# First product of the second network for two of three token blocks in seven half products, with converted weights and some results kept in scratch memory

## The chip, the cores and the metric

The kernel runs on one core of a Trainium2 chip. A core has TensorE (matrix products, results into the 8 banks of PSUM), VectorE, ScalarE and GpSimd (elementwise work), and SP, whose queue issues most transfers between the chip's memory and SBUF. The metric is the device time of one execution: 579.11 us before the change, the median of three (578.52 to 579.46).

## What is computed

Attention over 2 batches, 8 heads and 768 positions; its output is laid out as 1536 tokens by 512. Two networks follow:

```python
x = attention(q, k, v)                # 1536 x 512
h = ((x @ w1) * (x @ w2)) @ w3        # w1, w2: 512 x 1024, w3: 1024 x 1024
x = h @ w_out                         # 1024 x 512, the first network's result
h = x @ w_in                          # 512 x 2048: the first product of the second network
g = h * np.clip(h + 3.0, 0.0, 6.0) / 6.0
y = g @ w_out2                        # 2048 x 512: its second product
```

The results are float32. The weights arrive as 64-bit numbers.

## The kernel before

Tokens go in three blocks (j) of 512. A float32 operand is held as two tiles, a high part (`F32R`) and the remainder, and a product of two operands is three passes of TensorE (high x high, low x high, high x low), so a 128 x 128 by 128 x 512 term is three matmuls (`products`, L299).

Weights are converted on the chip (`convert`, L228): a load into a staging buffer (`raws`, four of them), two instructions on ScalarE (L261, L267), two on VectorE that assemble a float32 in one of four buffers `cs` (L276, L280), then the high part on ScalarE (L284) and the low part on GpSimd (L288), both into a slot of the big tile `arena` or of one of the later tiles.

The first network runs block by block, eight steps each: `ab` (L532) makes two products of 12 matmuls in banks 4 and 5, multiplies them on VectorE and splits the result, and `acc1` (L548) accumulates it through the merged weights into banks 0 to 3. `x2_out` (L553) turns a finished block into the second network's input, four tiles with high and low parts. The attention of later blocks runs between these steps, in banks 6 and 7.

The second network takes 16 column tiles for each block. `hu` (L567) makes one tile of `h`, 4 terms or 12 matmuls in bank 4 or 5; ScalarE adds 3 and cuts at zero (L575), VectorE applies the minimum and multiplies (L579), and `split` (L517) makes the high part on ScalarE (L519) and the low part on VectorE (L524). `acc2` (L586) multiplies the tile of two steps earlier by its output weights, 12 matmuls, three into each of banks 0 to 3, which accumulate over 16 tiles. `y_out` (L591) writes a finished block. All 32 weight tiles of the second network stay in SBUF; the first eight slots of these (`late`) open when the attention's buffers close.

The order of the instructions is written by a planner. Each operation is put down with an engine, an assumed duration, a due time, the keys it reads and writes, and `Graph.schedule` (L100) lays out a list for each engine: what is ready goes, the earliest due first. On the chip each engine works through its list in order and waits where an operand isn't there.

Of the kernel before, what the change touches and what calls it, by code (L numbers as in the profile page):

```python
# [22 lines left out]
F32 = mybir.dt.float32  # L23
# [32 lines left out]
A_LATE = A_W2 + 8  # L56
N_RAW, N_C = 4, 4
# [105 lines left out]
def build(tc, qd, kw, vw, kt, vt, consts, wp_in, w12_in, w2_in, out):  # L163
# [5 lines left out]
    psp = tc.tile_pool(name="ps", bufs=1, space=bass.MemoryType.PSUM)  # L169
    pool = main.__enter__()  # L170
    pp = psp.__enter__()
    ar = pool.tile([P, A_N, 2, TB], F32R, name="arena")
# [27 lines left out]
    def open_tiles(cm, name, side, s0):  # L200
# [19 lines left out]
    def take(name, n):  # L220
        t = turn[name] % n
        turn[name] += 1
        return t
# [4 lines left out]
    def convert(due, src, s, pieces=1, banks=None, lo="pool", n_raw=N_RAW):  # L228

# [12 lines left out]
        if n_conv[0] <= LOD:  # L242
            lo = "dve"
        bk = banks[take("cb", len(banks))] if banks else None
        for i in range(pieces):
# [24 lines left out]
            else:  # L270
# [12 lines left out]
            g.op("act", 180 + 450 * f, due - 2 * us,  # L283
                 lambda cf=cf, e=e: nc.scalar.activation(out=slot(s)[:, 0, e], in_=cf, func=AF.Copy),  # L284
                 [kci] + [kc] * (pieces > 1), [("t", s, 0)])
            eng = nc.gpsimd if lo == "pool" else nc.vector
            g.op(lo, 60 + 1230 * f if lo == "pool" else 150 + 540 * f, due - 1.3 * us,
                 lambda cf=cf, e=e, eng=eng: eng.tensor_tensor(  # L288
                     out=slot(s)[:, 1, e], in0=cf, in1=slot(s)[:, 0, e].bitcast(F32), op=ALU.subtract),
                 [kci, ("t", s, 0)] + [kc] * (pieces > 1), [("t", s, 1)], True)  # L290
# [8 lines left out]
    def products(due, terms, out_ap, b, reads, start=True, stop=True, writes=None):  # L299


        def fn():
            n = 0
            for lhs, rhs in terms:
                for a, c in PASSES:
                    nc.tensor.matmul(  # L306
                        out=out_ap, lhsT=lhs(a), rhs=rhs(c),
                        start=start and n == 0, stop=stop and n == 3 * len(terms) - 1,
                    )
                    n += 1  # L310

        g.op("pe", 684 * len(terms), due, fn, reads, [("bank", b)])
# [254 lines left out]
    def hu(due, j, i, swin):  # L567
# [6 lines left out]
        t, u, gs = ta[n % 2], tg[n % 2], A_G + n % 3  # L574
# [11 lines left out]
    def acc2(due, i, gs, swout, cs_=range(4)):  # L586
        for c in cs_:
            terms = [(wslice(gs, c * P), lambda h: slot(swout)[:, h, :])]
            products(due + c, terms, bank[c], c, both(swout) + both(gs), i == 0, i == NFC2 - 1)

    def y_out(due, j, c, halves=False):  # L591
# [3 lines left out]
        for n, eng in enumerate(("act", "dve") if halves else ("act",)):  # L595
# [3 lines left out]
            def fn(eng=eng, e=e):  # L599
                if eng == "act":  # L600
                    nc.scalar.activation(out=o[:, e], in_=bank[c][:, e], func=AF.Copy, scale=1.0 / 6.0)
                else:
                    nc.vector.tensor_scalar(
                        out=o[:, e], in0=bank[c][:, e], scalar1=1.0 / 6.0, scalar2=None, op0=ALU.mult
                    )
# [4 lines left out]
            g.op(eng, 480 if w == TB else 290, due, fn, [("bank", c)], [("c", c % N_C, n)] + [("c", c % N_C)] * (n == 0))  # L610
# [34 lines left out]
    with tc.manual_schedule():  # L645
# [63 lines left out]
        for i in range(2):  # L709
# [3 lines left out]

        slots = [A_LATE + i for i in range(8)] + [w12(i) for i in range(2 * NFC)] + [A_WP + i for i in range(NFC)]
        g.op("late", 1, 0, lambda: open_tiles(att_cm, "late", "right", A_LATE), (),
             att_keys + [k for i in range(8) for k in both(A_LATE + i)])
        wslots = [(slots[2 * i], slots[2 * i + 1]) for i in range(NFC2)]

        acc1_last = pend
        order = [(j, i) for j in range(NBLK) for i in range(NFC2)]  # L720
        done = []
        first = True
        conv_next = 0

        def conv_to(n):
            nonlocal conv_next
            while conv_next < min(n, NFC2):
                i = conv_next
                dl = d2_of(i)
                convert(dl - 8 * us, w2_in[i], wslots[i][0])  # L730
                convert(dl - 4 * us, w2_in[NFC2 + i], wslots[i][1])
                conv_next += 1

        def d2_of(i):
            return T2 + (2 * i) * GRP


        conv_to((8 + 2 * NFC) // 2)
        for n, (j, i) in enumerate(order):
            gs = hu(due, j, i, wslots[i][0])  # L740
            due += GRP
            done.append((j, i, gs))
            if first:
                acc1(due, acc1_last[1], acc1_last[2])
                x2_out(due, acc1_last[0])
                due += GRP
                first = False
                conv_to(NFC2)
            if n >= 2:
                pj, pi_, pg = done[n - 2]  # L750
                acc2(due, pi_, pg, wslots[pi_][1])
                due += GRP
                if pi_ == NFC2 - 1:
                    for c in range(4):
                        y_out(due, pj, c)
        for c in range(4):
            for pj, pi_, pg in done[-2:]:
                acc2(due, pi_, pg, wslots[pi_][1], [c])
                due += GRP / 4
            y_out(due, NBLK - 1, c, c == 3)  # L760
        for _, i in g.schedule():
            g.ops[i][3]()
        for cm in reversed(pools):
            cm.__exit__(None, None, None)
        psp.__exit__(None, None, None)
# [68 lines left out]
```

## Time and profile before

| | |
|---|---|
| median of three runs | 579.11 us |
| span of the profiled execution | 577.1 us |
| outside the span | 2.0 us (of the median) |
| TensorE busy | 549.4 us, 3080 matmuls recorded |
| VectorE, ScalarE, GpSimd busy | 308.4, 258.7, 161.2 us |
| share of the chain of waits on TensorE | 84% |

The trace is of one execution, whose own time is known by its span alone. Instructions are named by engine, line and tiles (`out<-in`, without buffer numbers). A matmul's busy time overlaps with its neighbours', so the pace of TensorE is read from the starts of successive groups. A VectorE or GpSimd instruction that has begun and waits for its turn at SBUF counts as busy.

### The profile page before, as it was taken

The numbers are of one execution on the slowest core, as the hardware profiler recorded it, in microseconds if no ns is written. First come the engines' busy times: TensorE is split into PE (matmuls) and PEld (weight loads), VectorE is DVE, ScalarE is ACT, GpSimd is POOL, SyncE is SP. The second block draws the span as 40 slices with busy tenths as digits, with TensorE's granted clock in tenths as the row PEclk, the third lists the DMA queues.
The fourth block names the chain that finished last, engine by engine and source line by source line (L and its number), as shares of the span: only waits on it lengthen the run. The fifth ranks groups of instructions, "written<-read, shape, count | busy, mean of one in ns | idle before, by whom it ended". The sixth has DMA issues, their size and how long they took to land.

```text
span 577.1 us, 7851 instructions
## 1 busy us (share of the span) xinstructions
PE 549.4 (95%) x3080; PEld 448.1 (78%) x3080; DVE 308.4 (53%) x416; ACT 258.7 (45%) x435; POOL 161.2 (28%) x130
## 2 busy tenths in 40 slices
PE   0689999999999999999999999999999999999997
PEld 0467778887878887878888888888888888888885
DVE  5899978857793336478976862222222222222221
ACT  2788877446531122386777652223222122322222
POOL 0578656794430022254633440000000000000000
PEclk9989999999999999999999999999999999999999
DMA  8999773655443010025553310000100000100002
GB/s 310 380 359 337 214 272 110 203 183 203 149 133 108 21 50 28 1 76 172 187 181 114 110 36 2 1 1 1 73 0 1 0 1 0 74 0 1 0 1 73
DMA packets 27709, 60.16 MB, mean 104 GB/s; under 512 B 2441, under 2 KB 11913, under 8 KB 27673
## 3 DMA queue, kind: packets, MB, share of 16 engines
q1 hardware_dynamic: 27528, 59.53, 31.6%
q8 instruction: 24, 0.39, 0.3%
q10 hardware_dynamic: 144, 0.13, 0.1%
q14 instruction: 13, 0.10, 0.0%
HBM read 54.90 MB, written 3.15 MB: 101 GB/s over the span
## 4 chain that ended last, share of the span: by engine, by line
PE 84%; DMA 9%; DVE 4%; ACT 1%; SPq 1%; issue 1%; ACTq 0%; DVEq 0%
PE bank L306 81%; DMA raw<-in_wp_dram 7%; PE bank L489 1%; DMA kall<-in_kw_dram 1%; PE bank L474 1%; PE bank L427 1%; DVE c L280 1%; DMA raw<-in_w_dram 1%; SPq L226 1%; DVE sc L438 0%; DVE st L458 0%; DVE bank L276 0%; ACT sc L455 0%; DVE arena L506 0%; DVE st L459 0%
## 5 line engine op out<-in xcount | busy, mean ns | idle before, releaser
L306 PE MATMUL bank<-arena 128*128 128x512 f32 x1344 | 323.1, 395 | 0.9 <-DVE arena L640 0.7
L306 PEld LDWEIGHTS bank<-arena 128*128 128x128 f32 x1344 | 251.6, 189 | 56.3 <-issue 1.4
L579 DVE SCALAR_TENSOR_TENSOR tg<-ta,bank 128x512 f32<-128x512 f32 x48 | 33.1, 689 | 141.8 <-ACT ta L575 141.8
L306 PE MATMUL bank<-arena,w 128*128 128x512 f32 x432 | 103.4, 392 | 0.0
L575 ACT ACTIVATE ta<-bank,three 128x512 f32<-128x512 f32 x48 | 33.0, 688 | 144.7 <-PE bank L306 144.7
L306 PEld LDWEIGHTS bank<-arena,w 128*128 128x128 f32 x432 | 80.5, 188 | 17.1 <-issue 0.3
L288 POOL TENSOR_TENSOR arena<-c,arena 128x512 fp32r<-128x512 f32 (+1 forms) x50 | 65.4, 1321 | 64.6 <-ACT arena L284 64.6
L519 ACT ACTIVATE arena<-tg 128x512 fp32r<-128x512 f32 x72 | 45.5, 632 | 62.0 <-DVE tg L543 31.3
L524 DVE TENSOR_TENSOR arena<-tg,arena 128x512 fp32r<-128x512 f32 x68 | 52.0, 764 | 34.0 <-ACT arena L519 33.9
L276 DVE SCALAR_TENSOR_TENSOR c<-c,raw 128x512 uint32<-128x512 uint32 x48 | 49.4, 1048 | 3.4 <-ACT raw L267 3.3
L280 DVE SCALAR_TENSOR_TENSOR c<-raw,c 128x512 uint32<-128x512 uint32 x48 | 48.3, 1019 | 0.2
L267 ACT ACTIVATE raw<-raw 128x512 uint32<-128x512 uint32 (+1 forms) x72 | 47.2, 660 | 0.0
L261 ACT ACTIVATE c<-raw 128x512 f32<-128x512 f32 x48 | 31.8, 667 | 19.4 <-DMA raw<-in_w_dram 16.7
L543 DVE TENSOR_TENSOR tg<-ta,bank 128x512 f32<-128x512 f32 x24 | 16.5, 686 | 44.9 <-PE bank L306 43.7
L454 POOL TENSOR_TENSOR sc<-sc,st 128x960 f32<-128x960 f32 x12 | 21.9, 1829 | 51.5 <-DVE st L452 51.5
L306 PE MATMUL bank<-late,arena 128*128 128x512 f32 x144 | 34.6, 389 | 0.0
L306 PE MATMUL bank<-w,arena 128*128 128x512 f32 x144 | 34.6, 389 | 0.0
L306 PE MATMUL bank<-arena,late 128*128 128x512 f32 x144 | 34.4, 389 | 0.0
L284 ACT ACTIVATE arena<-c 128x512 fp32r<-128x512 f32 (+1 forms) x50 | 29.8, 605 | 4.8 <-DVE c L280 2.8
L306 PEld LDWEIGHTS bank<-arena,late 128*128 128x128 f32 x144 | 27.0, 188 | 5.6
L306 PEld LDWEIGHTS bank<-late,arena 128*128 128x128 f32 x144 | 27.0, 188 | 5.6
L306 PEld LDWEIGHTS bank<-w,arena 128*128 128x128 f32 x144 | 27.0, 188 | 5.6
(48 smaller groups left out, 369.0 us busy)
## 6 DMA issues: line engine op xcount, KB each, us to landing
raw<-in_w_dram SPq DMA_DIRECT2D x48, 512.0 KB, 3.8
raw<-in_wp_dram SPq DMA_DIRECT2D x22, 512.0 KB, 7.2
vall<-in_vw_dram SPq DMA_DIRECT2D x24, 192.0 KB, 4.0
raw<-in_vt_dram SPq DMA_DIRECT2D x6, 512.0 KB, 4.1
qst<-in_q_dram SPq DMA_DIRECT2D x12, 256.0 KB, 3.6
out_dram<-c SPq DMA_DIRECT2D x11, 256.0 KB, 2.2
kall<-in_kw_dram SPq DMA_DIRECT2D x8, 320.0 KB
raw<-in_kt_dram SPq DMA_DIRECT2D x3, 512.0 KB
```

The source lines that it names most:

```text
L261: lambda uf=uf, wf=wf: nc.scalar.activation(out=uf, in_=wf[:, :, 1], func=AF.Copy, scale=2.0**-112),
L267: lambda lw=lw: nc.scalar.activation(out=lw, in_=lw, func=AF.Copy, scale=2.0**-29 * (1 - eps), bias=7.5 * eps - 0.5),
L276: lambda ui=ui, lw=lw: nc.vector.scalar_tensor_tensor(out=ui, in0=ui, scalar=3, in1=lw, op0=ALU.logical_shift_left, op1=ALU.bitwise_or),
L280: lambda ci=ci, ui=ui, hw=hw: nc.vector.scalar_tensor_tensor(out=ci, in0=hw, scalar=0x80000000, in1=ui, op0=ALU.bitwise_and, op1=ALU.bitwi ...
L284: lambda cf=cf, e=e: nc.scalar.activation(out=slot(s)[:, 0, e], in_=cf, func=AF.Copy),
L288: lambda cf=cf, e=e, eng=eng: eng.tensor_tensor(out=slot(s)[:, 1, e], in0=cf, in1=slot(s)[:, 0, e].bitcast(F32), op=ALU.subtract),
L306: nc.tensor.matmul(out=out_ap, lhsT=lhs(a), rhs=rhs(c), start=start and n == 0, stop=stop and n == 3 * len(terms) - 1,)
L454: lambda: nc.gpsimd.tensor_tensor(out=s8, in0=s8, in1=wide(0), op=ALU.subtract), [("st", i2)], skeys)
L519: g.op("act", 630, due, lambda: nc.scalar.activation(out=slot(s)[:, 0, :], in_=src_ap, func=AF.Copy), [src_key], [("t", s, 0)])
L524: lambda: eng.tensor_tensor(out=slot(s)[:, 1, :], in0=src_ap, in1=slot(s)[:, 0, :].bitcast(F32), op=ALU.subtract), [src_key, ("t", s, 0)], ...
L575: g.op("act", 600, due, lambda: nc.scalar.activation(out=t, in_=bank[b], func=AF.Relu, bias=three), [("bank", b), "three"], [("ta", n % 2)])
L579: lambda: nc.vector.scalar_tensor_tensor(out=u, in0=t, scalar=6.0, in1=bank[b], op0=ALU.min, op1=ALU.mult), [("bank", b), ("ta", n % 2)], ...
```

## The change

Token blocks 0 and 1 and the two halves of the inner dimension (512 = 2 x 256) form a 2 x 2 arrangement with two column tiles of `w_in` (tiles q and q + 8). Where the kernel before made four tiles of `h` from eight half products of 6 matmuls, the changed one makes seven half products of sums and differences of the operands (Strassen's scheme, in the form with fewer sums), for each of the 8 values of q. Block 2 is still computed by `hu`.

- `sums_of_x`: before the loop, GpSimd adds high and low parts of eight tiles of x, VectorE forms eight differences, and they are split again into the slots `A_W1` (of the first network's weights).
- `w_in_group(q)`: two converted tiles of `w_in`; GpSimd forms four half-width sums or differences of them in `tmps` 6 and 7; all four tiles are split into the slots `A_W2`. The plain two are also stored to scratch memory (`wi`).
- The loop: per q the half products 1, 5, 6, 2, 7, 4, 3 go to three of banks 4 to 7. Bank A collects 1, 6, 7 and 4, and ScalarE copies it out after 1, 6 and 7 (`copied`); bank B takes 2, bank C takes 5 and 3. VectorE adds the copies to the banks (`added`) for three of the four results; `gated` applies the activation and the split. Block 0's two results are accumulated in the next q (`acc2`, 24 matmuls); block 1's two are stored to scratch (`gj`).
- The 16 output weight tiles are converted in place in the staging buffers, stored to scratch (`wo`), and fetched into 12 slots as needed.
- After the loop: block 2, whose `w_in` tiles are fetched back from scratch, and last the accumulation of block 1 in banks 4 to 7, whose 16 results are fetched back.

The number of instructions goes from 418 to 466 on VectorE, 438 to 486 on ScalarE and 132 to 180 on GpSimd; SP issues 253 transfers instead of 153.

```diff
-        for i in range(8):
+        for i in range(n):
             tiles[s0 + i] = p2.tile([P, 2, TB], F32R, name=f"{name}{i}")
+        for i in range(n_tmp):
+            tmps[i] = p2.tile([P, TB], F32, name=f"{name}_f{i}")
...
+    def spill(due, key, src_fn, reads):
+        d = spilled[key]
+        g.op("sp", 1300, due, lambda: nc.sync.dma_start(out=d, in_=src_fn()), reads, [key])
+
+    def fetch(due, s, key):
+        d = spilled[key]
+        g.op("sp", 1300, due, lambda: nc.sync.dma_start(out=slot(s).bitcast(F32), in_=d), [key], both(s))
+
+    def convert_out(due, src, key, lo="pool"):
+
+        r, c, parts = to_f32(due, src)
+        e, f, cf, keys = parts[0]
+        w = raws[r].bitcast(F32R).rearrange("p (two n) -> p two n", two=2)
+        kr = [("raw", r)]
+        to_hi_lo(due, 1, lambda: cf, keys, lambda: w[:, 0, :], lambda: w[:, 1, :], kr, kr, lo)
+        spill(due, key, lambda: raws[r].bitcast(F32).rearrange("p (two n) -> p two n", two=2), kr)
...
+        wo_slot = [A_LATE + i for i in range(N_LATE)] + [A_WP + i for i in range(NFC)]
+        n_wo = len(wo_slot)
+        tslot = {n: [A_W1 + 2 * (n - 1) + k for k in range(2)] for n in range(1, 5)}
+        ring = [A_G, A_G + 1, A_G + 2, A_X + NPAIR, A_X + NPAIR + 1]
...
+        def w_in_group(due, q):
+
+            w = [A_W2 + 4 * (q % 2) + i for i in range(4)]
...
+            for out, ko, x, kx, op, y, ky in (
+                ((e, lo), ke, (b, lo), kb, ALU.add, (b, hi), kb),
+                ((e, hi), ke, (e, lo), ke, ALU.subtract, (a, lo), ka),
+                ((f, lo), kf, (a, lo), ka, ALU.subtract, (b, lo), kb),
+                ((f, hi), kf, (a, hi), ka, ALU.subtract, (e, hi), ke),
+            ):
+                tensors(due, *(lambda v=v: v[0]()[:, v[1]] for v in (out, x, y)), op, kx, ky, ko, "pool", 0.5)
+            for i, (x, kx) in enumerate(src):
+                s = w[i]
+                to_hi_lo(due, 1, x, [kx], lambda s=s: slot(s)[:, 0, :], lambda s=s: slot(s)[:, 1, :],
+                         [("t", s, 0)], [("t", s, 1)], "dve" if i == 3 else "pool")
+                if i < 2:
+                    spill(due, ("wi", 2 * q + i), lambda s=s: slot(s).bitcast(F32), both(s))
...
+        PAIRS = {
+            1: (0, 0, [A_X, A_X + 1]), 2: (0, 1, [A_X + 2, A_X + 3]),
+            3: (3, 1, [A_X + NPAIR + 2, A_X + NPAIR + 3]), 4: (1, 1, tslot[4]),
+            5: (2, 0, tslot[1]), 6: (2, 1, tslot[2]), 7: (3, 0, tslot[3]),
+        }
...
+        def copied(due, b, f):
+            g.op("act", 600, due, lambda: nc.scalar.activation(out=tmps[f], in_=bank[b], func=AF.Copy),
+                 [("bank", b)], [("f", f)])
+
+        def added(due, b, f, o):
+            g.op("dve", 690, due,
+                 lambda: nc.vector.tensor_tensor(out=tmps[o], in0=bank[b], in1=tmps[f], op=ALU.add),
+                 [("bank", b), ("f", f)], [("f", o)])
+            return lambda: tmps[o], ("f", o)
...
+        sums_of_x(due)
+        for n in range(NFC2):
+            convert_out(due, w2_in[NFC2 + tile_of(n)], ("wo", n))
+        w_in_group(due, 0)
+        w_in_group(due, 1)
+        prev = []
+        for q in range(NFC):
+            bA, bB, bC = (4 + (3 * q + i) % 4 for i in range(3))
...
+            step(1, bA, True)
+            copied(due, bA, 0)
+            step(5, bC, True)
+            filled()
+            step(6, bA, False)
+            copied(due, bA, 1)
+            filled()
+            step(2, bB, True)
+            h11 = added(due, bB, 0, 3)
+            prev.append((2 * q, gated(due, *h11)))
+            step(7, bA, False)
+            copied(due, bA, 2)
+            h22 = added(due, bC, 2, 4)
+            filled()
+            gated(due, *h22, spilled_as=2 * q + 1)
+            step(4, bA, False)
+            prev.append((2 * q + 1, gated(due, lambda b=bA: bank[b], ("bank", bA))))
+            filled()
+            step(3, bC, False)
+            h12 = added(due, bC, 1, 5)
+            gated(due, *h12, spilled_as=2 * q)
+            if q + 2 < NFC:
+                w_in_group(due, q + 2)
...
+        for m, n in enumerate(order):
+            s = A_W2 + m % 8
+            fetch(due, s, ("wi", n))
+            gs = hu(due, NBLK - 1, s, ring[take("gs", len(ring))])
...
+        for n in range(NFC2):
+            s = A_W1 + n % 8
+            fetch(due, s, ("gj", n))
+            if n < NFC2 - 2:
+                acc2(due, n, s, at[n], b0=4)
```

The names in the pieces of order below: `arena` is the big tile (slots of x, of results and of weights), `bank4` to `bank7` take the first product, `bank0` to `bank3` the second, `w20` to `w27` are the slots `A_W2`, `late_f0` to `late_f7` the buffers `tmps`. A number behind a tile's name with an underscore is only its place in memory.

On TensorE, in the second network of the program before, one group of 12 for `hu` and one for `acc2` alternate:

```order
L306 MATMUL bank4_79<-arena_61 128x512 x12
L306 MATMUL bank0_75<-late5_2059,arena_61 128x512 x3
L306 MATMUL bank1_76<-late5_2059,arena_61 128x512 x3
L306 MATMUL bank2_77<-late5_2059,arena_61 128x512 x3
L306 MATMUL bank3_78<-late5_2059,arena_61 128x512 x3
L306 MATMUL bank5_80<-arena_61 128x512 x12
```

In the changed program, the same engine in the loop at q = 1, from the end of its product 6 (bank A is bank 7):

```order
L338 MATMUL bank7_132<-arena_111,w26_711 128x512 x6
L338 MATMUL bank2_127<-late0_2196,arena_111 128x512 x3
L338 MATMUL bank3_128<-late0_2196,arena_111 128x512 x3
L338 MATMUL bank4_129<-arena_111,w24_709 128x512 x6
L338 MATMUL bank7_132<-arena_111,w27_712 128x512 x6
L338 MATMUL bank0_125<-late1_2197,arena_111 128x512 x3
L338 MATMUL bank1_126<-late1_2197,arena_111 128x512 x3
L338 MATMUL bank7_132<-arena_111,w25_710 128x512 x6
```

Between the first two groups in bank 7 (products 6 and 7) stand 12 matmuls; between the last two (7 and 4) stand six. ScalarE copies the bank in each of these gaps.

On ScalarE, in the program before, near the end of the conversions (second network, block 0):

```order
L575 ACTIVATE ta0_70<-bank4_79,three_74 128x512
L284 ACTIVATE arena_61<-c3_69 128x512
L519 ACTIVATE arena_61<-tg0_72 128x512
L575 ACTIVATE ta1_71<-bank5_80,three_74 128x512
L519 ACTIVATE arena_61<-tg1_73 128x512
```

In the changed program, about a half of q = 1; L823 are the copies out of bank A, L292 the high parts of weights, L838 and L552 the activation and the high part of a result:

```order
L292 ACTIVATE w23_708<-late_f7_2207 128x512
L264 ACTIVATE c1_117<-raw2_114 128x512
L270 ACTIVATE raw1_113<-raw1_113 128x512
L823 ACTIVATE late_f1_2201<-bank7_132 128x512
L552 ACTIVATE arena_111<-tg1_123 128x512
L292 ACTIVATE w26_711<-late_f6_2206 128x512
L270 ACTIVATE raw2_114<-raw2_114 128x512
L292 ACTIVATE w24_709<-c2_118 128x512
L823 ACTIVATE late_f2_2202<-bank7_132 128x512
L838 ACTIVATE ta0_120<-late_f3_2203,three_124 128x512
```

The copies now stand between conversions and high parts of weights, some of which wait for GpSimd (`late_f6`, `late_f7`).

On SP's queue, before the last attention units, in the program before (loads into the staging buffers between the attention's):

```order
L226 DMA raw1_63<-in_w2_dram 128x512
L226 DMA vall2_98<-in_vw_dram 96x512
L226 DMA vall3_99<-in_vw_dram 96x512
L226 DMA raw3_65<-in_w2_dram 128x512
L226 DMA raw2_64<-in_w2_dram 128x512
L226 DMA raw0_62<-in_w2_dram 128x512
L226 DMA kall1_95<-in_kw_dram 128x4x160
```

The same place in the changed program:

```order
L237 DMA vall2_148<-in_vw_dram 96x512
L237 DMA vall3_149<-in_vw_dram 96x512
L309 DMA wo1_64<-raw2_114 128x1024
L237 DMA raw2_114<-in_w2_dram 128x512
L309 DMA wo0_63<-raw1_113 128x1024
L237 DMA raw1_113<-in_w2_dram 128x512
L309 DMA wo3_66<-raw0_112 128x1024
L237 DMA raw0_112<-in_w2_dram 128x512
L309 DMA wo2_65<-raw3_115 128x1024
```

Here each staging buffer is stored (`wo`) before it is loaded again; nine such stores stand ahead of the load of `kall1` that came after three loads before.

## Rows read from the trace of the kernel before

**Rows 1.** The chain of waits in order of time, from 245 us: start us, us, what

```profile
245.41 327.72 PE bank L306 x1443
```

**Rows 2.** The timeline, 350 to 366 us: start us, us, engine, line, operation, tiles, count

```profile
352.63 2.88 PE L306 MATMUL bank<-arena 128*128 128x512 f32 x12
352.89 0.69 ACT L575 ACTIVATE ta<-bank,three 128x512 f32<-128x512 f32 x1 [3.36 <-PE bank L306]
353.62 0.69 DVE L579 SCALAR_TENSOR_TENSOR tg<-ta,bank 128x512 f32<-128x512 f32 x1 [3.36 <-ACT ta L575]
...
355.36 2.88 PE L306 MATMUL bank<-arena,w 128*128 128x512 f32 x12
```

**Rows 3.** The page's head: span; busy us (share of the span) and instructions

```profile
span 577.1 us, 7851 instructions
...
PE 549.4 (95%) x3080; PEld 448.1 (78%) x3080; DVE 308.4 (53%) x416; ACT 258.7 (45%) x435; POOL 161.2 (28%) x130
```

**Rows 4.** Busy time by stretch; columns as in the first line

```profile
core 0: us, PE busy (x) PEld busy (x) DVE busy (x) ACT busy (x) POOL busy (x), PEclk, DMA share, GB/s
0.00:50.00 50.00, 28.71 (x243) 22.32 (x245) 39.39 (x62) 32.64 (x58) 27.56 (x30) 0.97 1.00 350
190.00:220.00 30.00, 30.00 (x221) 24.25 (x221) 11.44 (x18) 5.78 (x9) 4.36 (x3) 1.00 0.11 34
250.00:310.00 60.00, 60.00 (x266) 49.71 (x265) 49.66 (x56) 44.57 (x78) 29.66 (x22) 1.00 0.55 169
```

**Rows 5.** Groups by line and form: busy us, mean ns, idle before

```profile
L519 ACT ACTIVATE arena<-tg 128x512 fp32r<-128x512 f32 x72 | 45.5, 632 | 62.0 <-DVE tg L543 31.3 <-DVE tg L579 30.6
...
L541 ACT ACTIVATE ta<-bank 128x512 f32<-128x512 f32 x24 | 14.3, 594 | 35.4 <-PE bank L306 35.3
...
L288 POOL TENSOR_TENSOR arena<-c,arena 128x256 fp32r<-128x256 f32 x4 | 2.9, 728 | 14.5 <-ACT arena L284 14.5
```

**Rows 6.** The timeline, 297 to 330 us, VectorE and GpSimd

```profile
297.13 2.56 POOL L288 TENSOR_TENSOR w<-c,w 128x512 fp32r<-128x512 f32 x2 [3.13 <-ACT w L284]
...
298.50 0.69 DVE L543 TENSOR_TENSOR tg<-ta,bank 128x512 f32<-128x512 f32 x1 [2.15 <-PE bank L306]
...
301.36 0.68 DVE L280 SCALAR_TENSOR_TENSOR c<-raw,c 128x512 uint32<-128x512 uint32 x1
301.96 1.28 DVE L276 SCALAR_TENSOR_TENSOR c<-c,raw 128x512 uint32<-128x512 uint32 x2
...
323.75 1.60 POOL L288 TENSOR_TENSOR w<-c,w 128x512 fp32r<-128x512 f32 x1 [3.70 <-ACT w L284]
324.13 1.77 DVE L276 SCALAR_TENSOR_TENSOR c<-c,raw 128x512 uint32<-128x512 uint32 x1
...
325.31 1.74 POOL L288 TENSOR_TENSOR arena<-c,arena 128x512 fp32r<-128x512 f32 x1
```

**Rows 7.** Groups by line, 250 to 310 us, VectorE alone

```profile
L280 DVE SCALAR_TENSOR_TENSOR c<-raw,c 128x512 uint32<-128x512 uint32 x20 | 19.8, 1001 | 0.0
L276 DVE SCALAR_TENSOR_TENSOR c<-c,raw 128x512 uint32<-128x512 uint32 x20 | 18.1, 928 | 2.0 <-ACT raw L267 2.0
L524 DVE TENSOR_TENSOR arena<-tg,arena 128x512 fp32r<-128x512 f32 x8 | 9.4, 1171 | 0.5 <-ACT arena L519 0.5
```

**Rows 8.** The timeline of ScalarE, 250 to 310 us

```profile
271.82 0.68 ACT L261 ACTIVATE c<-raw 128x512 f32<-128x512 f32 x1 [1.21 <-DMA raw<-in_w_dram]
272.41 0.58 ACT L541 ACTIVATE ta<-bank 128x512 f32<-128x512 f32 x1
...
279.39 0.60 ACT L541 ACTIVATE ta<-bank 128x512 f32<-128x512 f32 x1 [0.51 <-PE bank L306]
...
295.96 0.57 ACT L541 ACTIVATE ta<-bank 128x512 f32<-128x512 f32 x1
```

**Rows 9.** Transfers by line: KB each, median us from issue to landing

```profile
raw<-in_w_dram SPq DMA_DIRECT2D x48, 512.0 KB, 3.8
...
out_dram<-c SPq DMA_DIRECT2D x11, 256.0 KB, 2.2
```

More of the change, by code (lines that the diff above doesn't have):

```diff
@@ L56 @@
 A_LATE = A_W2 + 8
+N_LATE, N_TMP = 4, 8
 N_RAW, N_C = 4, 4
@@ L282, in convert @@
                  keys + [ku] * bool(banks), [kci] + [kc] * (pieces > 1 and i == 0 and bool(banks)), not banks)
[L283 to L290, printed above, removed]
+            out.append((e, f, cf, [kci] + [kc] * (pieces > 1)))
@@ new lines, in convert @@
+    def convert(due, src, s, pieces=1, banks=None, lo="pool", n_raw=N_RAW):
+        if n_conv[0] < LOD:
+            lo = "dve"
+        r, c, parts = to_f32(due, src, pieces, banks, n_raw)
+        for e, f, cf, keys in parts:
+            to_hi_lo(due, f, lambda cf=cf: cf, keys, lambda e=e: slot(s)[:, 0, e], lambda e=e: slot(s)[:, 1, e],
+                     [("t", s, 0)], [("t", s, 1)], lo)
+    def spill(due, key, src_fn, reads):
+        d = spilled[key]
+        g.op("sp", 1300, due, lambda: nc.sync.dma_start(out=d, in_=src_fn()), reads, [key])
@@ L297, in build, with products @@
     PASSES = ((0, 0), (1, 0), (0, 1))
-    def products(due, terms, out_ap, b, reads, start=True, stop=True, writes=None):
+    def products(due, terms, out_ap, b, reads, start=True, stop=True, skip=False):
         def fn():
@@ L722, in build @@
[L722 to L740, printed above, removed]
-            due += GRP
[L742 to L745, printed above, removed]
-                due += GRP
[L747 to L751, printed above, removed]
+        g.op("late", 1, 0, lambda: open_tiles(att_cm, "late", "right", A_LATE, N_LATE, N_TMP), (),
+             att_keys + [k for i in range(N_LATE) for k in both(A_LATE + i)] + [("f", i) for i in range(N_TMP)])
@@ new lines, in build, with half_product @@
+        PAIRS = {
+            1: (0, 0, [A_X, A_X + 1]), 2: (0, 1, [A_X + 2, A_X + 3]),
+            3: (3, 1, [A_X + NPAIR + 2, A_X + NPAIR + 3]), 4: (1, 1, tslot[4]),
+            5: (2, 0, tslot[1]), 6: (2, 1, tslot[2]), 7: (3, 0, tslot[3]),
+        }
+        def half_product(due, q, n, b, start):
+            i, h, xs = PAIRS[n]
+            s = A_W2 + 4 * (q % 2) + i
+            terms = [(wslice(s, h * 2 * P + k * P), lambda c, x=xs[k]: slot(x)[:, c, :]) for k in range(2)]
+            products(due, terms, bank[b], b, both(s) + [k for x in xs for k in both(x)], start, skip=not start)
@@ new lines, in copied, with gated @@
+        def copied(due, b, f):
[6 more added lines that the diff above has]
+            return lambda: tmps[o], ("f", o)
+        def gated(due, h, kh, spilled_as=None):
+            n = chain["n"]
+            chain["n"] += 1
+            t, u = ta[n % 2], tg[n % 2]
+            gs = ring[take("gs", len(ring))]
+            g.op("act", 690, due, lambda: nc.scalar.activation(out=t, in_=h(), func=AF.Relu, bias=three),
+                 [kh, "three"], [("ta", n % 2)])
+            g.op("dve", 690, due,
+                 lambda: nc.vector.scalar_tensor_tensor(
+                     out=u, in0=t, scalar=6.0, in1=h(), op0=ALU.min, op1=ALU.mult),
+                 [kh, ("ta", n % 2)], [("tg", n % 2)], kh[0] == "f")
+            split(due, u, ("tg", n % 2), gs)
+            if spilled_as is not None:
+                spill(due, ("gj", spilled_as), lambda: slot(gs).bitcast(F32), both(gs))
+            return gs
@@ L759, in build @@
+        for c in range(4):
+            for n, s in last:
+                acc2(due, n, s, at[n], [c], b0=4)
                 due += GRP / 4
-            y_out(due, NBLK - 1, c, c == 3)
+            y_out(due, 1, c, c == 3, b0=4)
         for _, i in g.schedule():
@@ L764, in build @@
             cm.__exit__(None, None, None)
+        drp.__exit__(None, None, None)
         psp.__exit__(None, None, None)
```

126 lines of the change are left out of this document (104 added, 22 removed).

## Prediction

> **What bounds the kernel now.** I read the chain of waits first, then TensorE in order of time, then the other engines in the stretch that looks most like what the change makes. The chain of waits in order of time ends in one piece of 327.72 us that is nothing but TensorE's products, from 245.41 to the last output copy at 573.13 [rows 1]. The reader is to see that from there no other engine and no transfer sets the time. In order of time, a group of 12 matmuls takes 2.72 us (one starts at 352.63, the next at 355.36), whether its 12 go to one PSUM bank (the first product, `bank<-arena`) or three each to four banks (the second, `arena,w`): 0.2267 us a matmul, no price for a change of bank [rows 2]. So a matmul less from 245 on is worth 0.2267 us, as long as TensorE stays fed.
>
> **What goes.** Before, a pair of column tiles of the second network's first product takes 2 x 2 x 12 = 48 matmuls for two token blocks. After, seven half products of 6 matmuls each take 42. There are 8 such pairs (the loop over q): 8 x 6 = 48 matmuls less. Block 2 and all of the second product keep theirs. 48 x 0.2267 = 10.88 us. The page has 549.4 us of TensorE's busy time in a span of 577.1 us [rows 3], but matmuls overlap there, so I count starts and not busy time. The runs' median is 579.11 us, 2.0 us over the profiled span; what lies around the span is untouched, so the sum goes against 579.11. With nothing lost: 568.2 us.
>
> **What is added, outside the loop.** Sixteen output weights are converted as before, but into the staging buffers and stored to scratch memory, so they need not wait for the attention buffers to close. In the order of the changed program they move ahead of the last attention units. There VectorE has 11.4 busy of 30 us, ScalarE 5.8, GpSimd 4.4 and DMA 0.11 of its time [rows 4]; 16 conversions at about 1.4 us of VectorE, 2 us of ScalarE and 1.3 us of GpSimd fit over the 70 us from 175 to 245. On SP's queue their stores stand ahead of the loads of the last attention units and wait for GpSimd there; with GpSimd at 4.4 of 30 us these waits are short. The eight sums of x and the first two weight groups fall into 250 to 310, from which those conversions have gone. I cost all this at nothing: TensorE covers it, and it is dense there already. If the cover fails, an activation chain comes late for its second product, at most by the 1.2 us that is the largest lateness found below; the ends are 0 and 2 us (two such), and I take 0, which is what the stretch now shows.
>
> **What is added, in the loop.** One period (one q) has 42 + 24 = 66 matmuls, 14.96 us. Against that stand, per period with a weight group:
> - ScalarE: 3 copies of a bank at 0.594, 4 relus at 0.69, 4 high parts of results at 0.632, 4 of weights at the same, 4 conversion steps at 0.68 [rows 2, 5, 8]: 1.78 + 2.76 + 2.53 + 2.53 + 2.72 = 12.3 us, 82%.
> - VectorE and GpSimd: where both read SBUF, they take turns. Two GpSimd subtractions began at 323.75 and 325.31 and the second ended at 327.05, with one VectorE instruction (324.13 to 325.90) between them [rows 6]: 3.30 us for work that alone is 1.28 + 1.28 + 0.68 (the two at 297.13 took 2.56). An instruction of VectorE that reads PSUM ran in its 0.69 beside these two (298.50). Back to back, VectorE starts one every 0.60 us (301.36, 301.96), since 0.08 of the 0.68 overlap [rows 6]. A period has 12 VectorE instructions with two SBUF inputs, 7.2 us, and on GpSimd three subtractions at 1.28 and four half-width ones at 0.728 [rows 5, 6], 6.8 us: 14.0 of 14.96 us, 94%. Four more VectorE instructions read PSUM (2.4 us). If these go beside GpSimd, as at 298.50, 14.0 is the bound; if the fixed order never lets them, it is 16.4.
> - DMA: about 52 transfers of 512 KB during the eight periods (32 stores of weights and results, 12 fetches, 8 loads), 27.3 MB in 7 x 14.96 + 12.2 = 117 us, 233 GB/s; the first 50 us moved 350 GB/s at a busy share of 1.00 [rows 4].
>
> None of these is over the period, but none leaves much. The nearest rows are 250 to 310, where the present kernel converts weights beside dense TensorE work: 48 VectorE instructions with two SBUF inputs (20 + 20 + 8) at 0.60 and 22 GpSimd subtractions at 1.28 make 57.0 of 60 us [rows 4, 6, 7], 95%; ScalarE is at 44.6 of 60, and TensorE lost nothing [rows 1, 4]. The Trainium skill (SBUF — State Buffer, Who interferes with whom) has that pair as one exclusive lock: a VectorE instruction with two SBUF inputs and a GpSimd instruction that reads SBUF block each other for the whole instruction, while one with a PSUM input doesn't take part. The rows agree on both [rows 6]; by that rule the loop needs 14.0 us and no more only where the order brings a PSUM instruction of VectorE beside each GpSimd instruction in time, which speaks for the first rival.
>
> **The new waits.** In each q, bank A collects products 1, 6, 7 and 4, and ScalarE must copy it out between them: 24 places where TensorE waits for a copy. Behind a waiting matmul everything of TensorE is queued, and so all of the end. What a copy needs is read from a present link: the next group starts at 352.63, the relu on the bank just finished at 352.89, so 0.26 us; the copy takes 0.594; the next engine follows a finished ScalarE instruction after 0.04 us (353.58 to 353.62): 0.89 us [rows 2, 5]. In the changed order 14 of the 24 places have 12 or more matmuls in between (2.72 us, 1.83 to spare), and 10 have six (1.36 us, 0.47 to spare); both kinds are in the piece of TensorE's order that the section on the change shows. So a loss needs ScalarE to be late. How late it is under load I read from the seven copies of a bank between 254 and 304. They recur every 36 matmuls, 8.16 us. The one at 279.39 waited for TensorE, so it was on time; counted from it, the one at 295.96 was 0.25 late, and the one at 272.41 was 1.18 late, queued behind a conversion that waited 1.21 us for its load [rows 8]. The other four were within 0.1. One in seven over 0.47, by 0.71: 10 x 0.71 / 7 = 1.0 us. ScalarE will be at 82% and not 74%, and GpSimd's results stand ahead of copies in its queue, so I take twice that, 2.0 us. The ends are 0 (nothing below: what is left of TensorE is dense now, so nothing else can shorten) and 7.1 us (all ten late by 0.71).
>
> The weights for a group are made a period ahead, and the accumulation of a result trails its product by about half a period; a lateness of a few us is covered there. A load is issued some 10 us ahead of its conversion in the changed order, against 3.8 us to land now [rows 9]; covered too, also at twice that. The last accumulation (block 1, from scratch) fetches eight groups of 2.72 us ahead; nothing lost. The tail after the last matmul is the same.
>
> Sum: 579.1 - 10.9 + 2.0 = 570.2 us.
>
> **Rivals.**
> - The pair of VectorE and GpSimd paces the loop in part: all instructions take turns, 16.4 us a period, 1.44 over, in the six periods with a weight group: 8.6 us, 576.8 us. For it: 94% of a period is booked already, and all queues are in fixed order. Against it: 95% cost nothing at 250 to 310, and the conversions have a period to slip.
> - Slower than before: the same pair runs at the durations it has under contention, VectorE first waiting for GpSimd and TensorE's copies then waiting in ScalarE's queue behind high parts of weights that GpSimd has not summed. 16 VectorE instructions at 0.69 [rows 2] and 7.0 us on GpSimd (4 x 0.728 + 3 x 1.35, which is 29.66 / 22 [rows 4, 5]) one after another make 18.0 us; 3.0 over, six times, is 18 us: 586 us. It decides from 10.9 / 6 = 1.8 us over a period, a period of 16.8 us. For it: conversions in 250 to 310 average 0.93 and 1.00 us instead of 0.68 [rows 6, 7]. Against it: that loss is the turn-taking itself, already counted.
> - The scratch memory holds it up. Nothing here stores at a high rate: a 256 KB output takes 2.2 us from issue to landing [rows 9]. If a 512 KB store occupies the queues twice as long as a load at 350 GB/s (3.0 against 1.5 us), 32 stores and 20 loads need 126 us, 9 more than the loop has: 577 us. Against it: that 2.2 us is mostly latency.
> - It doesn't save its matmuls, since half products of 6 start slower. Groups of 3 to a bank run at full rate now [rows 2], so I give this nothing.
>
> **How the numbers follow.** Forecast 0.60; its own range is 567.6 (568.2 less the 0.6 us that the runs scatter downwards) to 573.5 (with 5.3 lost, about half way between 2.0 and 7.1 and a little of the stretch before). First rival 0.15, scratch memory 0.08, slower 0.17. The range takes in the two at 577, with the 2.0 us of bank copies on top and scatter: 567.6 to 579.5. It leaves out the slower case. Under 0.2% (1.2 us) this kernel's measurement can't tell from no change. Faster: 0.60 + 0.15 + half of 0.08 = 0.79; the rest of the scratch case is near no change, 0.04; slower 0.17.
>
> **What would show it.** Right: 48 matmuls fewer; a period of q between 15 and 15.5 us on TensorE; short idle pieces on TensorE released by ScalarE's bank copies, 2 us in all; the chain of waits still one TensorE piece to the loop and one after it. Wrong: a period over 16 us, released by VectorE or GpSimd (first or second rival); fetches or loads as releasers, with a DMA share near 1.00 in the loop (third); TensorE idle before 309 us (the conversions moved forward cost something after all); or an idle sum on the bank copies far from 2 us, which would mean that I mis-sized ScalarE's lateness.

## The result and the profile after

The changed kernel takes 586.66 us (median of four, 585.60 to 587.12) against 578.82 us (578.12 to 579.46) beside it: ratio 1.0134, 95% interval 1.0119 to 1.0148. It is 1.3% slower; the forecast was 570.2 us. The profiled span is 585.1 us, 8.0 more than before [rows 3].

The page's head of the changed kernel, with the slices of TensorE and of its clock:

```profile
span 585.1 us, 8146 instructions
...
PE 541.2 (92%) x3032; PEld 441.3 (75%) x3032; DVE 345.5 (59%) x464; ACT 283.0 (48%) x483; POOL 217.5 (37%) x178
...
PE   0679999999999939969999999999999999999997
...
PEclk9999999999999978979999999999999999999999
```

48 matmuls fewer (3032, before 3080), as the change promises. The span is longer all the same, and the slices say where: from the 15th to the 18th (205 to 263 us) TensorE has gaps and a lower granted clock. The chain of waits ends in one piece again (start us, us, what):

```profile
261.79 1.15 PE bank L522 x32
262.94 318.49 PE bank L338 x1404
```

Before, that piece began at 245.41 [rows 1]. From 263 us on TensorE waits for nothing, though the loop and its scratch traffic lie there. The loop's pace in the timeline (start us, us, engine, line, operation, tiles, count):

```profile
352.77 1.52 PE L338 MATMUL bank<-late,arena 128*128 128x512 f32 x6
354.13 4.24 PE L338 MATMUL bank<-arena,w 128*128 128x512 f32 x18
...
367.73 1.52 PE L338 MATMUL bank<-late,arena 128*128 128x512 f32 x6
369.09 4.24 PE L338 MATMUL bank<-arena,w 128*128 128x512 f32 x18
```

The pattern recurs after 367.73 - 352.77 = 14.96 us, which is 66 matmuls at 0.2267 and nothing else. The loss lies ahead of it. By stretch:

```profile
core 0: us, PE busy (x) PEld busy (x) DVE busy (x) ACT busy (x) POOL busy (x), PEclk, DMA share, GB/s
...
190.00:220.00 30.00, 19.83 (x133) 15.76 (x133) 15.91 (x20) 12.53 (x22) 8.47 (x6) 0.88 0.69 214
220.00:250.00 30.00, 30.00 (x228) 24.14 (x226) 18.68 (x29) 12.80 (x22) 12.98 (x8) 0.95 0.56 172
250.00:262.00 12.00, 7.45 (x57) 5.88 (x57) 8.01 (x11) 4.77 (x8) 2.60 (x2) 0.72 0.19 73
```

190 to 220 was 30.00 of 30 at clock 1.00 before [rows 4]. What the engines waited for (us, times, longest), first TensorE from 165 to 265 us, then ScalarE and SP's queue from 165 to 262:

```profile
PE bank L522 <- ACT pt L514: 14.5, 3, 10.0
...
ACT c L264 <- DMA raw<-in_w_dram: 35.7, 13, 4.9
...
SPq L237 <- DMA wo<-raw: 47.0, 14, 7.7
SPq L309 <- POOL raw L295: 16.3, 8, 7.5
```

TensorE waits for an attention copy (`pt`, L514); ScalarE, ahead of that copy in its list, waits for a load of weights into a staging buffer; and SP, ahead of that load, waits until the store out of the same buffer has landed. The chain of waits shows one such turn (start us, us, what):

```profile
208.32 5.11 DMA wo<-raw
213.48 4.12 DMA raw<-in_w_dram
217.68 0.66 ACT c L264
218.34 0.50 ACT pt L514
218.88 1.98 PE bank L522 x32
```

The store lands, the buffer is loaded again, ScalarE makes the first conversion step and then the copy. By then TensorE has stood for 9.95 us.

### The profile page after: what moved, and what is told of

It is laid out like the page before. It is cut to its first block, busy times and chain, and to the rows that moved or that the text cites. A ratio compares the mean times of both kernels' runs of the same rounds, so it can differ in the third digit from the quotient of the medians.

```text
span 585.1 us, 8146 instructions
## 1 busy us (share of the span) xinstructions
PE 541.2 (92%) x3032; PEld 441.3 (75%) x3032; DVE 345.5 (59%) x464; ACT 283.0 (48%) x483; POOL 217.5 (37%) x178
## 4 chain that ended last, share of the span: by engine, by line
PE 76%; DMA 11%; DVE 4%; POOL 3%; ACT 2%; issue 2%; SPq 1%; POOLq 0%; ACTq 0%; DVEq 0%
PE bank L338 72%; DMA wo<-raw 5%; DMA raw<-in_w_dram 4%; PE bank L522 2%; DMA kres<-in_kt_dram 1%; DMA qst<-in_q_dram 1%; PE bank L507 1%; PE bank L460 1%; POOL arena L295 1%; DVE st L491 1%; DVE c L283 1%; POOL raw L295 1%; POOL sc L497 1%; SPq L237 1%; ACT sc L488 1%
## 5 line engine op out<-in xcount | busy, mean ns | idle before, releaser
L338 PE MATMUL bank<-arena 128*128 128x512 f32 x1152 | 278.3, 395 | 1.1 <-DVE arena L673 0.7
L338 PEld LDWEIGHTS bank<-arena 128*128 128x128 f32 x1152 | 215.6, 189 | 48.5 <-issue 1.4
L338 PE MATMUL bank<-arena,w 128*128 128x512 f32 x816 | 197.1, 392 | 0.0
L338 PEld LDWEIGHTS bank<-arena,w 128*128 128x128 f32 x816 | 153.3, 189 | 32.4 <-issue 0.3
L552 ACT ACTIVATE arena<-tg 128x512 fp32r<-128x512 f32 x72 | 44.9, 627 | 33.1 <-DVE tg L576 16.9
L295 POOL TENSOR_TENSOR arena<-c,arena 128x512 fp32r<-128x512 f32 (+1 forms) x34 | 42.4, 1260 | 32.5 <-ACT arena L292 32.5
L295 POOL TENSOR_TENSOR w<-c,w 128x512 fp32r<-128x512 f32 x24 | 34.2, 1428 | 25.9 <-ACT w L292 25.9
L612 DVE SCALAR_TENSOR_TENSOR tg<-ta,bank 128x512 f32<-128x512 f32 x16 | 11.0, 689 | 50.2 <-ACT ta L608 50.2
L295 POOL TENSOR_TENSOR raw<-c,raw 128x512 fp32r<-128x512 f32 x16 | 23.3, 1472 | 37.6 <-ACT raw L292 33.8
L608 ACT ACTIVATE ta<-bank,three 128x512 f32<-128x512 f32 x16 | 11.0, 687 | 48.9 <-PE bank L338 48.9
L497 POOL TENSOR_TENSOR sc<-sc,st 128x960 f32<-128x960 f32 x12 | 22.2, 1850 | 23.1 <-DVE st L493 22.1
L522 PE MATMUL bank<-pt,vall 120*64 120x64 f32 x384 | 15.5, 240 | 14.5 <-ACT pt L514 14.5
L487 POOL TENSOR_TENSOR sc<-sc,st 128x960 f32<-128x960 f32 x12 | 23.0, 1919 | 15.5 <-DVE st L485 15.5
```

The costliest lines, as they stand in the source:

```text
L295: lambda: e.tensor_tensor(out=lo(), in0=src(), in1=hi().bitcast(F32), op=ALU.subtract),
L338: nc.tensor.matmul(out=out_ap, lhsT=lhs(a), rhs=rhs(c), start=start and n == 0, stop=stop and n == 3 * len(terms) - 1, skip_group_check=skip,)
L487: lambda: nc.gpsimd.tensor_tensor(out=s8, in0=s8, in1=wide(0), op=ALU.subtract), [("st", i2)], skeys)
L497: lambda: nc.gpsimd.tensor_tensor(out=s8, in0=s8, in1=wide(1), op=ALU.mult), [("st", i2)], skeys)
L522: nc.tensor.matmul(out=bank[b0][h * D : (h + 1) * D, p * P + x * QT : p * P + (x + 1) * QT], lhsT=vall[vi[x]][0:NK, (2 * p + h) * D : (2 * ...
L552: g.op("act", 630, due, lambda: nc.scalar.activation(out=slot(s)[:, 0, :], in_=src_ap, func=AF.Copy), [src_key], [("t", s, 0)])
```

## The experiments

Theory A: the turn of a staging buffer (store, landing, reload) holds up the lists. It comes from one line of the planner. What follows on the same engine is taken to be ready after 35 ns, and SP's transfers counted as such: a reload was planned 35 ns after the store's slot of 1.3 us, where this trace has 5.1 us from issue to landing (median of 14). The rivals are in the expectations. Times are medians, each beside the kernel before on the same chip; kernels that ran on different chips are compared by their ratios to it.

**Landing in the plan (x1).**

```diff
-  at = t + ns + (0 if same and e == "pe" else 35 if same else self.LAT.get(e, 40))
+  at = t + ns + (0 if same and e == "pe" else 35 if same and e != "sp" else self.LAT.get(e, 40))
```

> The changed kernel, with one thing altered in the planner: a transfer that SP issues after another SP transfer of the same buffer is assumed to be possible 2.1 us after the first (as for the other engines) and no longer 0.035 us. Nothing else is different; the same transfers and conversions are made. Theory A (the reload of a staging buffer stands at the head of SP's and ScalarE's lists until the store before it has landed, and the attention's loads and copies stand behind it): TensorE idle between 190 and 262 us falls from 14.5 us to 5 or less, its granted clock there returns to 1.00, and the time is 568 to 574 us. Theory B (sixteen conversions beside the last attention units cost VectorE, GpSimd and ScalarE too much in whatever order): 583 to 587 us, as before the alteration. Theory C (the scratch traffic itself slows transfers and TensorE): the same 583 to 587.

569.11 us, ratio 0.9836 (0.9821 to 0.9851), as A says; the granted clock is 1.00 in all stretches from 160 to 440 us. The work of the changed kernel in another order is 1.6% faster than the kernel before. In the kernel before, the same line changes no engine's list, so this isn't a gain that was open to it already. The last piece, and all of TensorE's waits from 165 to 265 us:

```profile
247.66 316.10 PE bank L338 x1392
```

```profile
PE bank L338 <- ACT arena L535: 0.7, 1, 0.7
PE bank L522 <- DVE pt L512: 0.2, 1, 0.2
PE bank L338 <- DVE arena L539: 0.2, 1, 0.2
```

**A longer landing in the plan (x2).** As x1, and `spill` is given a latency of 4500 ns, used in place of `LAT` both for its due time and for when its readers are ready.

> As the run before, and the planner also assumes 4.5 us (instead of 2.1) from the end of a store's issue to its landing, near the 5.0 us of the trace. Theory A: the rest of the idle time goes too, and the time is the 48 matmuls under the kernel before, 578.8 - 10.9 = 567.9, range 566.5 to 570. Theories B and C: 583 to 587.

570.47 us, ratio 0.9854 (0.9838 to 0.9871). B and C fall again, but my 567.9 (566.5 to 570) was missed. The intervals of x1 and x2 overlap. The longer figure wasn't the truer one either: it came from the changed kernel's order, and the same stores land elsewhere in another time (from 165 to 262 us, first the changed kernel, then x1: KB each, median us from issue to landing):

```profile
wo<-raw SPq DMA_DIRECT2D x14, 512.0 KB, 5.1
...
wo<-raw SPq DMA_DIRECT2D x15, 512.0 KB, 2.7
```

x1's plan has 1.3 + 2.1 us for this, x2's 1.3 + 4.5, and in x2's trace it is 3.8.

**The conversions put back behind the attention (x4, x4b).** The loads of the sixteen conversions read a key that the opening of the late tiles writes; x4b has x1's line as well.

```diff
-            convert_out(due, w2_in[NFC2 + tile_of(n)], ("wo", n))
+            convert_out(due, w2_in[NFC2 + tile_of(n)], ("wo", n), after=["open"])
```

> The changed kernel, but the sixteen output weight conversions may begin only when the attention's buffers have closed (about 246 us), as in the kernel before. Theory A with an empty loop: 568 to 572 us, no idle time ahead of 246. Rival (the pair VectorE and GpSimd is booked out from 246 on: 16 conversions are 16 x (2 x 0.60 + 1.28) = 40 us of turns more, against 5% of spare time): idle time on TensorE moves into 270 to 360, 20 to 30 us of it, and the time is 590 to 600.

608.57 us (one execution): theory A's 568 to 572 fails here, and it is worse than the rival's 590 to 600. TensorE is at 30.00 of 30 us from 190 to 250. From 250 to 360 it waits, most for ScalarE's high parts (L552, 18.3 us in 3). In the chain of waits from 255 to 362 us the loads of weights have 32.4% and the landings of the stores 20.5%: the turns now come later.

> The changed kernel with the conversions kept behind the attention (the run that took 608.6 us), and now with the planner's 2.1 us as well. It tells how much of those 608.6 is order and how much is lack of room on VectorE and GpSimd. Theory A alone (order is all): 568 to 573 us. Room is short too (40 us of VectorE and GpSimd turns more between 246 and 360, where 5% were spare): 583 to 593 us, TensorE waiting for x's sums, weight groups or bank copies between 290 and 345.

595.46 us (one execution). So 13 us of it was that line of the planner, but some 26 more than x1 remain, a little above the 583 to 593 for a lack of room. With this planner the move ahead of the attention's end pays, and what was bad was its order; other orders behind the attention were not tried.

**That part alone (x3b, x3c).** The tail of the kernel before, with `wo` through scratch; x3c has x1's line. (A first build, x3, passed `hu` other operand tiles by my mistake, which makes other waits; its 604.25 us isn't used.)

```diff
+        for i in range(NFC2):
+            convert_out(due, w2_in[NFC2 + i], ("wo", i))
...
-                convert(dl - 4 * us, w2_in[NFC2 + i], wslots[i][1])
+                fetch(dl - 4 * us, wslots[i][1], ("wo", i))
```

> The kernel before (no half products, its own order of the second network) with one part of the change: the sixteen output weight tiles are converted in the staging buffers, stored to scratch and fetched into their slots when those open; planner as in the changed kernel. Theory A: the loss of the stretch 190 to 262 without the gain, 14.5 us idle and about 4 us of lower clock: 578.5 + 18.5, range 593 to 602 us. Theory D (the loss belongs to the combination with the sums of x and the weight groups): 578 to 584.

596.17 us, ratio 1.0308 (1.0267 to 1.0350). SP waits for landings of these stores 46.1 us in 14 times from 165 to 262 us, as long as in the changed kernel (47.0).

> The run before with the planner's 2.1 us between two SP transfers of one buffer. Theory A: nearly all of that loss goes, as it did with the half products (569.1 against 586.7): 578 to 583 us. If the assumed landing had helped the changed kernel through something in the loop and not in this stretch, it would stay at 593 to 602.

581.54 us, ratio 1.0059 (1.0036 to 1.0082). Both as A says: the loss comes with the sixteen conversions through scratch memory, without any half product, and most of it goes with the planner's line.

**A pause by itself (x5).** The kernel before, a copy of `pt[0]` issued 20 times for one attention unit.

> The kernel before, with one attention copy (the one at 206.4 us, for which TensorE waits 0.2 us later) made 20 times over, to hold TensorE once for about 10 us near 207 as the changed kernel was held at 209 to 219. If an idle piece costs its own length: 578.5 + 10.0 = 588.5, granted clock 1.00. If the granted clock falls behind a pause, as the 0.88 and 0.95 of the changed kernel suggest: 1.5 to 3 us more, 590 to 592, with groups of 24 matmuls at 6.5 to 6.9 us in place of 5.6 behind the pause.

589.99 us (one execution), 11.6 more. It held the next unit's copy, at 219.9 and not 206.4. The last piece, 245.41 before [rows 1], begins 11.06 us later, at 256.47 (327.68 us long); the pause is 9.94. Behind it, and ahead of it for comparison, in TensorE's timeline:

```profile
206.80 1.15 PE L491 MATMUL bank<-pt,vall 120*64 120x64 f32 x32
207.88 1.66 PE L306 MATMUL bank<-arena 128*128 128x512 f32 x6
209.37 5.60 PE L306 MATMUL bank<-arena,w 128*128 128x512 f32 x24
214.90 1.05 PE L427 MATMUL bank<-kall,qst 64*64 64x120 f32 x32
...
232.50 1.98 PE L491 MATMUL bank<-pt,vall 120*64 120x64 f32 x32 [9.94 <-ACT pt L483]
234.40 3.70 PE L306 MATMUL bank<-arena,w 128*128 128x512 f32 x12
238.03 1.05 PE L427 MATMUL bank<-kall,qst 64*64 64x120 f32 x32
```

The group of 32 takes 1.90 us to the next start, and 1.08 ahead of the pause. Twelve matmuls take 3.63, where 24 took 5.53 ahead of it, so 2.77 for twelve. That is 0.8 + 0.9 = 1.7 us for the granted clock (0.83 in this profile from 220 to 250, 1.00 from 190 to 220). The start of the last piece shows 1.1 of it, since this execution was 0.4 us ahead at 207 (206.80, in the kernel before 207.24).

**The stores on another queue (x6).** The changed kernel, all lists the same, the `wo` stores issued by GpSimd.

> The changed kernel with its own order on every engine; only the queue of the sixteen weight stores is GpSimd's in place of SP's, right behind the subtraction that makes the data. It parts the two things that theory A holds together. SP's list (a load that waits for a landing holds up the stores of the other three buffers): in the trace these conversions begin every 5.5 us, which is one landing and one store one after the other; with the stores off that list the four buffers turn at once, one conversion every 3 to 3.5 us, TensorE idle 0 to 6 us: 569 to 578 us. ScalarE's list alone (the conversion's first instruction stands before the attention's copy, whatever SP does): 583 to 588 us.

586.78 us, ratio 1.0135 (1.0115 to 1.0156). My 569 to 578 failed: taking the stores off SP's list, where they stood behind waiting loads, gives nothing back. SP still waits for landings, longer than in the changed kernel:

```profile
SPq L237 <- DMA wo<-raw: 71.3, 14, 13.2
```

So either the landing in each turn is the cause, or the place of the conversions in the lists of ScalarE and VectorE.

**No landing in the turn (x10).** The changed kernel's lists, the same stores at the same places, read from a tile that nothing rewrites there. So the reload of a staging buffer waits for GpSimd's subtraction, and no more for the store to land.

```diff
-        spill(due, key, lambda: raws[r].bitcast(F32).rearrange("p (two n) -> p two n", two=2), kr)
+        spill(due, key, lambda: slot(A_WP + 4).bitcast(F32), kr)
```

> The changed kernel with every engine's list as it was; the sixteen weight stores take as many bytes at the same places of SP's list, but from a tile of the arena that nobody rewrites there, so that the staging buffer's reload waits for GpSimd's subtraction and no more for a landing (the stored output weights are other data, so the last product's values change, and nothing else). The run with the stores on GpSimd's queue left the time at 586.8, so SP's list of stores was not the cause. Theory A': the landing of the store inside each buffer's turn (5 us of 9 to 10) starves ScalarE's fixed list: idle on TensorE between 190 and 262 falls from 14.5 to 0 to 5 us, 569 to 576 us. Theory E (ScalarE's and VectorE's lists put these conversions too early in any case; the load alone, 3.6 to 4 us, holds them up): 580 to 587.

567.44 us, ratio 0.9806 (0.9778 to 0.9835). Its last piece; then TensorE's largest wait from 165 to 265 us, and, to 262, ScalarE's on the loads and SP's on the buffers:

```profile
243.51 318.49 PE bank L338 x1404
```

```profile
PE bank L522 <- ACT pt L514: 0.7, 1, 0.7
...
ACT c L264 <- DMA raw<-in_w_dram: 10.9, 6, 3.4
...
SPq L237 <- POOL raw L295: 31.7, 14, 4.5
```

The last piece is the changed kernel's, to the hundredth: 318.49 us and 1404 records. It only begins 262.94 - 243.51 = 19.43 us earlier. As the stores moved the same bytes (median 5.6 us to landing), neither the traffic nor the conversions' places in the lists are the cause: theories C and E fall, A' stands. The cause is the landing inside the buffer's turn, in lists that were laid out without it.

These 19.4 us can be followed in the changed kernel's TensorE timeline:

```profile
218.88 1.98 PE L522 MATMUL bank<-pt,vall 120*64 120x64 f32 x32 [9.95 <-ACT pt L514]
220.79 6.83 PE L338 MATMUL bank<-arena,w 128*128 128x512 f32 x24
227.55 1.05 PE L460 MATMUL bank<-kall,qst 64*64 64x120 f32 x32
...
254.83 1.98 PE L522 MATMUL bank<-pt,vall 120*64 120x64 f32 x32 [3.86 <-ACT pt L514]
256.74 2.93 PE L338 MATMUL bank<-arena 128*128 128x512 f32 x6
259.46 1.64 PE L507 MATMUL bank<-con,sc 128*120 128x128 f32 x8
```

Waits: 14.5 less x10's 0.7, 13.8 us. Lower clock, start to start against the usual 1.08, 5.53, 1.08 and 1.36: 0.83 + 1.23 + 0.83 + 1.36, and 0.6 for the last group (1.64 long, elsewhere 1.04): 4.8 us. That is 18.6 of 19.4. Of the rest, 0.4 us lies ahead of 168 us, where x10's execution was that much ahead before any of this (a group starts at 167.97 and not 168.40), and 0.4 between 199 and 205 us, where TensorE waits 0.22 for VectorE's scores.

**ScalarE's margin in the loop (x7).** x1, and each of the 24 bank copies issued twice.

> The kernel of 569.1 us (planner with the landing), each of the 24 bank copies of the loop made twice by ScalarE, to see what the 2.0 us of the prediction's term were about. In its trace every copy begins 0.2 us after its product and takes 0.60, against 1.36 us to the bank's next use at the ten short places: 0.5 us to spare; a second copy adds 0.5 to 0.6. If the copies are on time as that trace has it: 0 to 1.5 us more, 569 to 570.6. If ScalarE's lateness under load is what the prediction said (a late copy in seven by 0.7 us, more at a higher load): 4 us or more, 573 to 577.

572.21 us, ratio 0.9882 (0.9865 to 0.9898): by the ratios 2.7 us more than x1, between the two. The last piece is 318.63 us, 2.5 longer than in x1. In the timeline a short place and the next starts:

```profile
349.19 1.52 PE L338 MATMUL bank<-late,arena 128*128 128x512 f32 x6
350.67 1.65 PE L338 MATMUL bank<-arena,w 128*128 128x512 f32 x6
352.16 1.52 PE L338 MATMUL bank<-late,arena 128*128 128x512 f32 x6
```

1.48 us where single copies leave 1.36: 0.12 late. The reading of 0.5 us to spare holds (0.20 + 1.23 for two copies + 0.04 = 1.47). The six matmuls behind take 1.49, so 0.13 more: 0.25 a place, and ten such places make the 2.5 us. Why the second six are longer stays open.

**GpSimd's margin (x8).** x1, the half-width sums three times over in six groups.

> The kernel of 569.1 us; the four half-width sums of a weight group are made three times over in six of the eight groups, 8 x 0.74 = 5.9 us more on GpSimd for each. It tests the sum by which the prediction called VectorE and GpSimd 94% booked (14.0 of 14.96 us in a period). If they take turns to the full, as that sum has it: 19.9 us a period from then on, less what the weights are ahead (up to two periods and 5%): 569 + 5 to 25, 574 to 594 us. If the turns overlap or the booking was too high: within 1.5 us of 569.

572.14 us, ratio 0.9883 (0.9863 to 0.9902): by the ratios again 2.7 us more than x1, between the two. From 249.04 to the end of the products are 318.0 us, 1.9 more than in x1. Between 316 and 427 us of this run 72 VectorE instructions have two SBUF inputs, 43.2 us at 0.60; GpSimd has 18 at 1.28 and 64 at 0.74, 70.4 us. That is 113.6 of 111 us, and TensorE was idle for 1.0 of them: booked a little over the full, the turns cost a little. In x1 the same stretch holds 75 of VectorE's, and 18 and 20 of GpSimd's: 82.8 us, 75%.

## Why the prediction was wrong, point by point

- **48 matmuls, 10.88 us: right.** With the landing out of the turn the time is 578.83 - 567.44 = 11.4 us under the kernel before; by that run's interval it is 9.6 to 12.9 us, and the 0.5 over lies inside it.
- **"Added, outside the loop", costed at 0 with ends 0 and 2 us: the step that failed.** It said: "On SP's queue their stores stand ahead of the loads of the last attention units and wait for GpSimd there; with GpSimd at 4.4 of 30 us these waits are short." It asked when a store could begin, and not when its buffer could be loaded again. Behind the store stood a reload of the same buffer; behind that SP's next transfers, ScalarE's conversion, the attention's copy and TensorE. Measured: 19.4 us, of which 13.8 waits and 4.8 clock. Both durations could be had: a 256 KB output landed in 2.2 us and a weight load in 3.8 [rows 9]; by an estimate at twice the output's time, a turn is 4.4 + 3.8 us and the conversion, and the planner had put the reload 35 ns behind the store. The share of busy engines that I read [rows 4] can't show it, since VectorE, ScalarE and GpSimd stand idle in such a wait. My end of 2 us came from lateness of copies in another stretch [rows 8] and bounded nothing here. "TensorE idle before 309 us" was the sign that I named for it.
- **Sum:** 579.1 - 10.9 + 2.0 had to be 578.8 - 11.4 + 19.4 = 586.8.
- **Bank copies, 2.0 us: too much.** They cost nothing in the changed kernel: the period is 14.96. The one copy in seven that was late [rows 8] stood behind a conversion whose load was late; from 263 to 440 us of the changed kernel ScalarE waits for such a load once, for 0.4 us.
- **The rival at 586 us has the right time by chance and the wrong cause.** It needed a period of 18 us, and the period is 14.96; the first rival (16.4) falls with it. My 94% for VectorE and GpSimd was the work of a period with a whole weight group in it; counted in x1's trace the loop has 75%, as the conversion steps of only four groups fall into those 111 us and the others were done ahead.
- **Scratch memory:** in the loop its transfers never released TensorE, and the stores there landed in 2.6 (`wi`) and 3.4 us (`gj`, medians of 16), no slower than the loads of weights (4.0). I priced it as a rate in the loop, and what cost was the time to land in a turn of four buffers ahead of it.

The Trainium skill (DMA: Bandwidth & Descriptors, Two DMAs through the same engine are not ordered) says that the issuing engine has to wait for the first transfer's completion where a second depends on it, and that sharing a queue is no substitute. The trace shows this wait: SP stands for landings, 47.0 us in 14 times. The planner's 35 ns left it out.

## What to carry to other kernels

When a change stores a buffer to memory and fills it again, work out the length of the whole turn (wait, store, landing, load, first use); then look what stands behind the reload in every list, to the engine that sets the end. That there are several buffers doesn't shorten it where one list waits for the landings in order: with four of them ScalarE's conversions began 5.0 us apart in the changed kernel (ten from 177.40 to 222.59), about a landing, and 3.7 us without the landing (x10, 174.87 to 208.22). A planner that treats two transfers of one queue as an engine's consecutive instructions hides that turn. An edit of that one line made the changed kernel faster than the one before it (569.1 us, 1.6%), while moving the part behind the attention made it worse (608.6 us).

## What the runs showed of the hardware that was not expected

- A pause of 9.94 us cost TensorE 11.6 us in all (x5, one execution). After the pause of 3.86 us in the changed kernel six matmuls took 2.72 us to the next start, 0.453 each, where 0.2267 is usual: half the pace, the lower of the clock's two levels, 1.2 and 2.4 GHz. The 0.88, 0.95 and 0.72 by stretch lie between the two, as means do.
- The time that a 512 KB store to scratch took to land varied with what was under way beside it. In the changed kernel one at 229.03, 7 us behind SP's last transfer, let the reload go 2.7 us later, at 231.75; one at 202.66, 0.8 us behind a load of 512 KB, took 5.16. From 165 to 262 us the median was 5.1 us there, 2.7 in x1, and 5.6 in x10, where it cost nothing. From GpSimd's queue it was 3.9 (x6), and nothing was gained.
